# Tile 2 moves behind weight row 3 on SyncE's DMA queue, and weight row 6 takes its place on ScalarE's queue

## The chip, the cores and the metric

The kernel runs on one core of one Trainium2 chip. The metric is the device time of one execution in microseconds (us). The kernel before took 1615.66 us in the median of its first 3 runs (1615.08 to 1616.13). Only one core is used, so there is no other core to compare with.

PE is TensorE (the matrix engine), ACT is ScalarE, DVE is VectorE, SP is SyncE. "SPq" and "ACTq" are the sequencers of SyncE and ScalarE, which issue the DMAs. The span is the time from the first to the last instruction of a profiled execution; it is about 1.8 us shorter than the time.

## The reference

The program is two rounds of two layers, on an input of 2048 rows by 1024 columns in bfloat16:

```python
x = x + attention(layernorm(x), wqkv, wo)   # 8 dilated positions, 32 heads of 32
x = x + swiglu(layernorm(x), w1, w3, w2)    # hidden size 3584
# ... and both once more, with the same weights
```

Nearly all of the time is in the matrix multiplications (PE is busy 1601.8 of 1614.1 us). This study is about the first 16 us alone: the first 512 rows of `x` (tiles 0 to 3 of 128 rows each, 256 KB a tile) are normalized and multiplied by the Q part of `wqkv`. That part is loaded in 8 rows of 128 x 1024 (256 KB each); "row 6" is the seventh.

## The kernel before

Operations are first recorded with estimated durations. A small scheduler inside the kernel then puts them into one order for each engine, and the kernel emits them in that order. So a moved transfer can also change the order of much later instructions. `queue="AQ"` means that ScalarE issues the transfer; otherwise SyncE does.

The opening, with cuts:

```python
def q_first():
    for hh in range(2):                      # tile 0 in two halves, one on each queue
        dma(128, x_sb[0][...], xin[:, 0, ...], [], [("x", 0, hh)], 0, queue="AQ" if hh else "SP")
    dma(256, x_sb[1][:], xin[:, 1, :], [], [...], 0, queue="AQ")
    rows = q_weights(0, "k", load=False)
    for kk in range(5):
        rows[2](kk)                          # weight rows 0 to 4, SyncE
    load_x(0, 3, 4)                          # tile 3, SyncE
    rows[2](5)
    rows[2](7)
    # ... averages of tile 0: half on DVE, half on ACT (writes "part")
    dma(256, x_sb[2][:], xin[:, 2, :], [("part", 0)], [...], 0, queue="AQ")     # tile 2
    # ... average of tile 1 on ACT (writes mean 1)
    rows[2](6, queue="AQ", after=[("mean", 1)])                                 # row 6
    # ... tiles 0 and 1: subtract the mean, transpose on PE, copy to `ce`
    # ... tiles 2 and 3: statistics on DVE, normalize, transpose on PE, copy to `xnT`
    # PE, tiles 0 and 1 (line 520): one row of weights after another, kk = 0 .. 7
    # PE, tiles 2 and 3 (line 534): 64 matmuls, all weight rows
    # ...
    wslots[1] = q_weights(1, "s")            # K weights: two blocks of 1 MB, SyncE
```

PE's program order in this stretch is: rows 0 to 5 for tiles 0 and 1 (rows 0 to 2 first for tile 0, then for tile 1), row 6, the transposes of tiles 2 and 3 (line 430), row 7, then the 64 matmuls of tiles 2 and 3. The DMAs share eight completion semaphores in turn, so a DMA is issued only once the one eight places earlier has landed (in the first profile tile 3 at 4.88 us after row 0 at 4.87, row 6 at 6.76 after row 2 at 6.74). Row 6's issue stands in ScalarE's instruction order, behind a copy of tile 0.

## Time and profile before

| | kernel before |
|---|---|
| span of the profiled execution | 1614.1 us |
| PE busy | 1601.8 us |
| PE waits over 0.15 us | 2 (0.77 us at the start, 1.16 us for row 6) |
| row 6: issued, landed | 6.76, 12.98 us |
| matmuls of tiles 2 and 3 (line 534) start | 15.67 us |

The page's own totals, busy us and share of the span:

```profile
span 1614.1 us, 19082 instructions
PE 1601.8 (99%) x7463; PEld 762.8 (47%) x7610; DVE 1122.1 (70%) x1906; ACT 331.1 (21%) x527; POOL 5.3 (0%) x28
```

In this profile, 147 of PE's 7610 matmuls left no record. So the waits, and not the busy sum, say what PE loses. The waits of PE over the whole execution (who waited for whom: us in total, times, longest):

```profile
PE bank L520 <- DMA slot<-in_A_wqkv_dram: 1.2, 1, 1.2
PE bank L285 <- PEq L756: 0.8, 1, 0.8
```

The timeline of PE from 4 to 24 us (start, duration, what; in brackets the idle time before it and what ended it):

```profile
3.71 1.49 PE L285 MATMUL bank<-const-bfloat16-1.0 128*128 128x512 bf16 x3
4.99 0.69 PE L430 MATMUL bank<-ident,xn 128*128 128x128 bf16 x8
...
7.29 4.57 PE L520 MATMUL bank<-hT,slot 128*128 128x128 bf16 x56
13.02 1.05 PE L520 MATMUL bank<-hT,slot 128*128 128x256 bf16 x8 [1.16 <-DMA slot<-in_A_wqkv_dram]
13.91 1.06 PE L430 MATMUL bank<-ident,xn 128*128 128x128 bf16 x16
14.80 1.04 PE L520 MATMUL bank<-hT,slot 128*128 128x256 bf16 x8
15.67 7.15 PE L534 MATMUL bank<-xnT,slot 128*128 128x256 bf16 x64
```

And the chain of waits in the same stretch (start, us, what):

```profile
5.21 1.15 ACT xn L458 x2
6.36 0.40 ACT hT L435
6.76 6.22 DMA slot<-in_A_wqkv_dram
12.98 0.05 issue
13.02 1.05 PE bank L520 x8
```

PE is busy 99% of the time, and after 13 us it waits for nothing. The one avoidable wait is row 6's. It is 0.07% of the time, so the question from the start is one of a microsecond. The chain shows how the wait comes about: ACT averages tile 1 and copies, then issues row 6 at 6.76, and the transfer takes 6.22 us. Other 256 KB pieces took 3.7 to 5.1 us.

How the DMA engines are shared is seen in the DMA view of two short windows (queue, kind: packets, MB, share of 16 engines; q1 is SyncE's queue, q10 ScalarE's). From 4.9 to 6.4 us:

```profile
q1 hardware_dynamic: 305, 0.56, 102.9%
```

From 7 to 8 us:

```profile
q10 hardware_dynamic: 125, 0.23, 60.7%
q1 hardware_dynamic: 95, 0.16, 43.8%
```

Tile 2 was issued on ScalarE's queue at 3.67 us. From 4.9 to 6.4 us it moves nothing, while SyncE's queue moves 0.56 MB; the SyncE pieces that land next, rows 1 to 4 (5.79 to 8.10 us), were issued before it. Tile 2's bytes move from near 7 us on (60.7% for ScalarE's queue, 43.8% for SyncE's). Why they wait, these runs do not settle; nor does the trace show whether tile 2 already stood in its queue then. The engines are full (from 4 to 16 us their mean share is 105%, at 388 GB/s), and 256 KB pieces land 0.67 us apart (row 3 at 7.42 to row 7 at 10.80, six pieces). Row 6's bytes move late. From 10.5 to 12 us they are the only ones on ScalarE's queue and share the engines with SyncE's:

```profile
q1 hardware_dynamic: 172, 0.35, 63.1%
q10 hardware_dynamic: 124, 0.23, 41.7%
```

### The profile page before, as it was taken

The numbers are of one execution on the slowest core, as the hardware profiler recorded it, in microseconds if no ns is written. First come the engines' busy times: TensorE is split into PE (matmuls) and PEld (weight loads), VectorE is DVE, ScalarE is ACT, GpSimd is POOL, SyncE is SP. The second block draws the span as 40 slices with busy tenths as digits, with TensorE's granted clock in tenths as the row PEclk, the third lists the DMA queues.
The fourth block names the chain that finished last, engine by engine and source line by source line (L and its number), as shares of the span: only waits on it lengthen the run. The fifth ranks groups of instructions, "written<-read, shape, count | busy, mean of one in ns | idle before, by whom it ended". The sixth has DMA issues, their size and how long they took to land.

```text
span 1614.1 us, 19082 instructions
## 1 busy us (share of the span) xinstructions
PE 1601.8 (99%) x7463; PEld 762.8 (47%) x7610; DVE 1122.1 (70%) x1906; ACT 331.1 (21%) x527; POOL 5.3 (0%) x28
## 2 busy tenths in 40 slices
PE   9999999999999999999999999999999999999999
PEld 6555544444444444444444444444444444444444
DVE  5898888889889888888898729884288832211211
ACT  5423322021211222113211032110321101101110
POOL 1000000000000000000000000000000000000000
DMA  9834755395548764858545487355873464454451
GB/s 314 231 102 149 225 170 170 117 225 170 171 136 249 194 193 130 218 166 250 172 139 159 161 243 229 125 172 176 250 225 119 156 183 156 144 174 152 156 164 45
DMA packets 350649, 285.80 MB, mean 177 GB/s; under 512 B 72288, under 2 KB 344928, under 8 KB 350560
## 3 DMA queue, kind: packets, MB, share of 16 engines
q1 hardware_dynamic: 349984, 283.67, 58.5%
q8 instruction: 59, 0.97, 0.3%
q10 hardware_dynamic: 576, 0.92, 0.2%
q14 instruction: 30, 0.25, 0.1%
HBM read 238.94 MB, written 29.36 MB: 166 GB/s over the span
## 4 chain that ended last, share of the span: by engine, by line
PE 99%; DMA 1%; issue 0%; ACT 0%; DVE 0%; ACTq 0%
PE bank L347 98%; PE bank L534 0%; DMA slot<-in_A_wqkv_dram 0%; DMA x<-in_A_x_dram 0%; PE bank L520 0%; ACT xn L458 0%; PE bank L430 0%; ACT L281 0%; ACT hT L435 0%; DVE x L699 0%; ACTq L458 0%
## 5 line engine op out<-in xcount | busy, mean ns | idle before, releaser
L347 PE MATMUL bank<-xnT,slot 128*128 128x512 bf16 x4955 | 1088.9, 379 | 5.3
L347 PEld LDWEIGHTS <-slot 128*128 128x128 bf16 x5056 | 518.1, 102 | 573.0
L347 PE MATMUL bank<-slot,hT 128*128 128x512 bf16 (+2 forms) x1812 | 387.3, 372 | 1.9
L669 DVE TENSOR_TENSOR hT<-sg,bank 128x512 bf16<-128x512 bf16 x224 | 153.6, 686 | 212.6 <-PE bank L347 196.3
L265 DVE TENSOR_TENSOR scr<-scr 128x1024 bf16<-128x1024 bf16 (+3 forms) x576 | 293.7, 540 | 2.1
L347 PEld LDWEIGHTS <-hT 128*128 128x128 bf16 x1848 | 178.6, 98 | 208.6
L667 ACT ACTIVATE sg<-bank 128x512 bf16<-128x512 f32 x224 | 133.8, 597 | 654.1 <-PE bank L347 613.9
L265 DVE TENSOR_TENSOR scr<-qT,kT 128x2048 bf16<-128x2048 bf16 x128 | 154.2, 1221 | 72.4 <-DMA kT<-qkv_d 70.6
L405 ACT CAST sgt<-bank 128x512 bf16<-128x512 f32 x184 | 107.7, 587 | 288.4 <-PE bank L347 271.6
L265 DVE TENSOR_TENSOR scr<-pA,vT 128x2048 bf16<-128x2048 bf16 x128 | 152.9, 1222 | 0.4
L699 DVE TENSOR_TENSOR x<-x,bank 128x512 bf16<-128x512 bf16 (+1 forms) x66 | 43.7, 670 | 122.6 <-PE bank L347 122.4
L347 PE MATMUL bank<-wo,oT 128*128 128x512 bf16 x502 | 112.6, 379 | 0.5
L313 DVE BATCH_NORM_STATS2 st<-x 128x6 f32<-128x512 bf16 x124 | 81.6, 680 | 12.1 <-DMA x<-in_A_x_dram 11.7
L347 PEld LDWEIGHTS <-oT 128*128 128x128 bf16 x512 | 50.1, 98 | 60.4
L644 DVE TENSOR_TENSOR x<-x,bank 128x512 bf16<-128x512 bf16 x64 | 43.9, 686 | 35.4 <-PE bank L347 33.9
L320 ACT ACTIVATE sd<-mv,epst 128x4 f32<-128x4 f32 (+1 forms) x17 | 5.1, 298 | 183.0 <-DVE mv L316 182.7
L604 DVE STREAM_TRANSPOSE pB<-pA 128x2048 bf16<-128x2048 bf16 x16 | 37.0, 2310 | 0.4
L627 DVE STREAM_TRANSPOSE pA<-pB 128x2048 bf16<-128x2048 bf16 x16 | 37.0, 2310 | 0.4
L667 ACT ACT_TABLE_LOAD x20 | 25.7, 1283 | 51.0 <-PE bank L347 50.8
L265 DVE TENSOR_TENSOR pA<-scr 128x256 bf16<-128x256 bf16 x128 | 35.8, 287 | 0.3
L265 DVE TENSOR_TENSOR oT<-scr 128x256 bf16<-128x256 bf16 x128 | 34.2, 289 | 0.1
L327 DVE TENSOR_SCALAR xn<-x,mv,rstd 128x1024 bf16<-128x1024 bf16 x62 | 30.9, 542 | 4.0 <-DMA xnT<-xn 3.7
(61 smaller groups left out, 211.2 us busy)
## 6 DMA issues: line engine op xcount, KB each, us to landing
slot<-in_B_w_dram SPq DMA_DIRECT2D x160, 1024.0 KB, 5.9
slot<-in_A_wqkv_dram SPq DMA_DIRECT2D x28, 1024.0 KB, 5.2
qkv_d<-sgt SPq DMA_DIRECT2D x92, 256.0 KB, 3.4
qT<-qkv_d SPq DMA_DIRECT2D x16, 512.0 KB, 5.2
slot<-in_B_w_dram SPq DMA_DIRECT2D x16, 512.0 KB, 5.7
kT<-qkv_d SPq DMA_DIRECT2D x14, 544.0 KB, 6.7
vT<-qkv_d SPq DMA_DIRECT2D x14, 544.0 KB, 5.2
out_dram<-x SPq DMA_DIRECT2D x31, 128.0 KB, 4.2
```

The lines of the kernel that those rows point to most:

```text
L265: return lambda _: nc.vector.tensor_tensor(o, a, b, op=op)
L313: dve(0.67, lambda _, hh=hh: nc.vector.bn_stats(st[q][:, j, hh, :], x_sb[n][:, hh * 512:(hh + 1) * 512]), [("x", n, hh)] + list(after), [( ...
L320: act(0.3, lambda _: nc.scalar.activation(sd[q][:, j0:j1], mv[q][:, j0:j1, 1], ACTF.Sqrt, bias=epst[:]), [("mv", q, j) for j in range(j0, ...
L327: dve(0.5, lambda _: nc.vector.tensor_scalar(xn[j][:], x_sb[n][:], mv[q][:, j, 0:1], rstd[q][:, j:j + 1], op0=ALU.subtract, op1=ALU.mult), ...
L347: nc.tensor.matmul(bank[a.bank][:, 0:ncol], lhsT=w, rhs=r, start=first and i == 0, stop=last and i == n - 1)
L405: evac(act, 0.59, lambda _, a=a, i=i, m=m: nc.scalar.copy(sgt[i][:, m % 2, :], bank[a.bank][:]), op, [], [("sgt", i, m % 2)], a)
L604: dve(2.31, lambda _: nc.vector.transpose(psmT[:].rearrange("p c d -> p (c d)"), psm[:].rearrange("p w s -> p (w s)")), allA, ["pB"])
L627: dve(2.31, lambda _: nc.vector.transpose(At[:].rearrange("p w s -> p (w s)"), AeT[:].rearrange("p c d -> p (c d)")), ["pB"], allA)
L644: evac(dve, t1(512), lambda _, xs=xs, a=a: nc.vector.tensor_tensor(xs, xs, bank[a.bank][:], op=ALU.add), op, [("x", n, hh)], [("x", n, hh) ...
L667: evac(act, 0.6, lambda _, i=i, a=ag: nc.scalar.activation(sg[i][:], bank[a.bank][:], ACTF.Silu), og, [], [("sg", i)], ag, table="silu")
L669: evac(dve, t1(512), lambda _, i=i, a=au, f=f: nc.vector.tensor_tensor(hT[:, f, :], sg[i][:], bank[a.bank][:], op=ALU.mult), ou, [("sg", i ...
L699: evac(dve, t1(cn), lambda _, xs=xs, a=a, cn=cn: nc.vector.tensor_tensor(xs, xs, bank[a.bank][:, 0:cn], op=ALU.add), op, [("x", n, hh)], [ ...
```

## The change

The intent is to issue row 6 three microseconds earlier without delaying anything that PE needs sooner. Tile 2 is needed later than row 4 by PE (from 13.91 us against 9.96), and row 6 can take tile 2's old place, right after ACT has been given its half of tile 0's average.

```diff
-        for kk in range(5):
+        for kk in range(4):
             rows[2](kk)
+        load_x(0, 2, 3)
+        rows[2](4)
         load_x(0, 3, 4)
         rows[2](5)
         rows[2](7)
 # ... (cut)
-        dma(256, x_sb[2][:], xin[:, 2, :], [("part", 0)], [("x", 2, 0), ("x", 2, 1)], 0, queue="AQ")
+        rows[2](6, queue="AQ", after=[("part", 0)])
 # ... (cut: average of tile 1)
-        rows[2](6, queue="AQ", after=[("mean", 1)])
```

## The prediction

> **What bounds the kernel.** TensorE. The page gives PE 1601.8 of 1614.1 us busy, granted clock 1.000. By the waits view PE waits only twice: 0.8 us for the program's start, and 1.16 us (11.86 to 13.02) for a DMA of a Q-weight row. All other gaps are under 0.06 us. So no change of the opening can be worth more than about 1.3 us of 1615 (0.08%), however it goes.
>
> **What the wait is.** In the timeline of the first 26 us PE works the Q weights row by row: row 3 from 9.08, row 4 from 9.96, row 5 from 10.83; row 6 could start at 11.70 but starts at 13.02. Row 6 is issued on ScalarE's queue at 6.76 us, behind the averaging of tile 1 and a copy, when SyncE's queue already holds row 5, row 7 and two 1 MB blocks; it lands at 12.98, 6.2 us later. The DMA engines are full (about 395 GB/s from 4 to 16 us), and the 256 KB pieces land in one sequence 0.67 us apart on either queue: row 3 7.42 (SyncE), row 4 8.10 (SyncE), tile 2 8.78 (ScalarE), tile 3 9.45, row 5 10.12, row 7 10.80 (SyncE). [...]
>
> **What the change does.** Nothing is added or removed: the same transfers, matmuls and copies. The built programs show PE's order unchanged until about matmul 860 of 7610. Each DMA waits for an earlier one on its completion semaphore (eight, in turn). Row 6 takes tile 2's issue, 3.67 us; tile 2 takes row 4's; row 4 gets the wait that tile 3 had (for row 0, landing at 4.87), tile 3 that of row 5, and so on. So I estimate, in steps of 0.67 us: tile 2 lands at 8.1 (was 8.78), row 6 at 8.8 (was 12.98), row 4 at 9.45 (was 8.10), tile 3 at 10.1, row 5 at 10.8, row 7 at 11.5.
>
> **On the critical path.**
> - Row 6's wait vanishes: gain up to 1.32 us.
> - Row 4 lands 0.5 us before PE wants it (9.96). Row 5 lands just when PE wants it (10.83): cost 0 to 0.2 us.
> - VectorE's statistics of tile 2 finish earlier but its next instruction, tile 3's, starts about 0.13 us later (10.01 to 10.15). Tiles 2 and 3 are normalized at about 12.35 and 13.0, when PE finishes row 6 (12.6) and tile 2's transposes (13.05): cost 0 to 0.1.
> - The 64 matmuls of tiles 2 and 3 start at about 14.4 instead of 15.67.
>
> **Later.** PE then runs about 1.2 us earlier against DMA and VectorE. The scheduler also reorders later work: the output-projection groups move by 8 matmuls in 9 of 16 places. Before, VectorE finished their input 0.6 to 4.3 us ahead of PE. Some slack shrinks, so I allow 0.2 us of new short waits.
>
> **Predicted time:** 1614.5 us, 1613.4 to 1615.8 (runs of the kernel before scatter by about 0.5 us either way). Faster by over 2%: 0.003; within 2%: 0.992; slower: 0.005.
>
> **What would show it.** PE's wait for a weight row near 12 us is gone or below 0.3 us; row 6 lands near 8.8; row 4 near 9.5; tile 3's statistics start near 10.15; the matmuls of the second half of the Q stage start near 14.4; PE's busy time stays 1601.8 and the span falls by about 1.1.
>
> **What would make it wrong.** Row 5 landing well after 10.83, turning row 6's wait into row 5's; tile 3 late, so that PE waits for its transposes; new waits of PE for VectorE or a DMA after 100 us, where slack was small and the order changed. Each costs at most a few us: even then, the verdict is the same.

## The result, and the profile after

The changed kernel took 1615.05 us in the median of 6 runs (1614.84 to 1615.30), the kernel before 1615.81 us in the same rounds (1614.98 to 1616.57). The ratio is 0.9996, with a 95% interval of 0.9983 to 1.0009: the same time by the 2% rule. A ratio is the mean time of one kernel's fast runs over that of the other's of the same rounds, so it is not quite the ratio of the medians.

The page's totals of the changed kernel:

```profile
span 1613.1 us, 19082 instructions
PE 1601.3 (99%) x7463; PEld 762.7 (47%) x7610; DVE 1122.3 (70%) x1906; ACT 329.6 (20%) x526; POOL 5.3 (0%) x28
```

All waits of its PE:

```profile
PE bank L285 <- PEq L757: 0.8, 1, 0.8
PE bank L430 <- DVE xn L472: 0.4, 1, 0.4
PE bank L521 <- DMA slot<-in_A_wqkv_dram: 0.2, 1, 0.2
```

The same timeline of PE (the changed kernel's line numbers are one higher here: 521 for 520, 535 for 534):

```profile
3.71 0.92 PE L285 MATMUL bank<-const-bfloat16-1.0 128*128 128x512 bf16 x3
4.53 0.72 PE L430 MATMUL bank<-ident,xn 128*128 128x128 bf16 x8
5.19 0.61 PE L521 MATMUL bank<-hT,slot 128*128 128x128 bf16 x8
5.96 0.62 PE L521 MATMUL bank<-hT,slot 128*128 128x128 bf16 x8 [0.16 <-DMA slot<-in_A_wqkv_dram]
6.96 0.66 PE L430 MATMUL bank<-ident,xn 128*128 128x128 bf16 x8 [0.39 <-DVE xn L472]
7.46 5.44 PE L521 MATMUL bank<-hT,slot 128*128 128x128 bf16 x64
12.74 1.06 PE L430 MATMUL bank<-ident,xn 128*128 128x128 bf16 x16
13.63 1.04 PE L521 MATMUL bank<-hT,slot 128*128 128x256 bf16 x8
14.51 7.15 PE L535 MATMUL bank<-xnT,slot 128*128 128x256 bf16 x64
```

The 56 matmuls before the wait and the 8 after it are now one run of 64, without a gap: row 6's wait is gone. The last group starts at 14.51 instead of 15.67, which is 1.16 us earlier, and the span is 1.0 us shorter. Two small waits are new, 0.16 us for row 1 and 0.39 us for tile 1's mean. Both stand before row 2. In this execution PE also began 0.46 us earlier (4.53 instead of 4.99): the last three of its ten warm-up matmuls on constants (line 285) took 0.92 us instead of 1.49. Tile 0 landed earlier too, at 3.08 us rather than 3.46, but that does not explain it alone: in profile c of the kernel before, below, tile 0 landed at 3.08 and PE began at 4.99. That the Q group is earlier by just the 1.16 us of the old wait is therefore partly chance: PE gained 0.46 us at the start and lost 0.55 in the two new waits. In the changed kernel's second profile PE began at 4.99, and the Q group at 14.82.

The chain of waits no longer contains a weight row:

```profile
6.55 0.36 DVE xn L472
6.92 0.05 issue
6.96 0.66 PE bank L430 x8
7.62 5.28 PE bank L521 x64
```

Where each piece landed, from the trace, beside the prediction:

| piece | before | predicted | changed kernel |
|---|---|---|---|
| tile 2 | 8.78 | 8.1 | 8.43 |
| row 6 | 12.98 | 8.8 | 8.62 |
| row 4 | 8.10 | 9.45 | 9.28 |
| tile 3 | 9.45 | 10.1 | 9.97 |
| row 5 | 10.12 | 10.8 | 10.63 |
| row 7 | 10.80 | 11.5 | 11.29 |

### The profile page after: what moved, and what is told of

It reads as the page before. It is cut to its first block, busy times and chain, and to the rows that moved or that the text cites. A ratio compares the mean times of both kernels' runs of the same rounds, so it can differ in the third digit from the quotient of the medians.

```text
span 1613.1 us, 19082 instructions
## 1 busy us (share of the span) xinstructions
PE 1601.3 (99%) x7463; PEld 762.7 (47%) x7610; DVE 1122.3 (70%) x1906; ACT 329.6 (20%) x526; POOL 5.3 (0%) x28
## 4 chain that ended last, share of the span: by engine, by line
PE 99%; issue 1%; DMA 0%; ACT 0%; DVE 0%; ACTq 0%
PE bank L347 98%; PE bank L535 0%; PE bank L521 0%; DMA x<-in_A_x_dram 0%; PE bank L430 0%; ACT L281 0%; DVE xn L472 0%; ACT xn L460 0%; DVE x L700 0%; ACTq L460 0%
```

## The experiments

Two questions were open. First, does the microsecond come from the opening alone, or also from the changed order of later work? Second, why did row 6 take 6.2 us, and why do the runs of the kernel before scatter by 1.6 us when those of the changed kernel scatter by 0.5? Each run below was timed in 5 rounds beside the kernel before (nine runs of it in each batch), except the last three.

### The changed kernel again

No edit.

> The changed kernel as it stands, for comparison on this chip. Theory A (the removed 1.16 us wait is passed on to the end nearly whole): 0.6 to 1.3 us below the kernel before; no PE wait for a weight row over 0.3 us. Rival B (the difference seen so far is chance; something later takes the gain back): within 0.4 us of the kernel before.

Measured: 1615.26 us (1615.09 to 1615.37); the kernel before 1615.63 us (1614.66 to 1617.65), ratio 0.9996 (0.9984 to 1.0009). PE has no wait for a row above 0.15 us. By the medians the gain is 0.37 us, which is the rival's range; by the means it is larger (0.56 us), because the kernel before has runs above 1617. So the changed kernel is not faster than the best runs of the kernel before: it lacks the slow ones.

### The opening alone, and the later order alone

For the first, the list that the scheduler made of the kernel before is kept, and only the two transfers are moved in it:

```diff
+        placed = pr.place()
+        # r6, x2, r3: the operations that load row 6, tile 2, row 3
+        placed.remove(r6)
+        placed[placed.index(x2)] = r6
+        placed.insert(placed.index(r3) + 1, x2)
+        x2.emit = lambda _: nc.sync.dma_start(x_sb[2][:], xin[:, 2, :])
-        for op in pr.place():
+        for op in placed:
             op.emit(op)
```

> The changed kernel's opening (tile 2 behind row 3 on SyncE's queue, row 6 in its place on ScalarE's), with every later instruction in the order of the kernel before. Theory A (only the opening counts): equal to the changed kernel within 0.3 us, so 0.6 to 1.3 us below the kernel before. Rival C (the later reordering brings or costs time): off the changed kernel by 0.5 us or more.

Measured: 1615.03 us (1614.87 to 1615.16), ratio to the kernel before 0.9995 (0.9983 to 1.0008). It is 0.23 us from the changed kernel's median in the same batch. In its profile PE waits for no row; up to 5.42 us it waits 1.0 us for tile 0, whose second half landed at 4.17 us instead of 3.64.

The second is the mirror image: the changed kernel's list, with tile 2 put back on ScalarE's queue and row 6 put back behind ACT's first copy and behind the first 1 MB block in the list.

> The opening of the kernel before (row 6 issued late on ScalarE's queue), with every later instruction in the order of the changed kernel. Theory A: equal to the kernel before within 0.3 us, PE waits about 1.2 us for row 6 near 12 us. Rival C: 0.5 us or more off the kernel before.

Measured: 1615.21 us (1614.92 to 1616.05), ratio 0.9998 (0.9985 to 1.0010). Its profiled run, the slowest of the five, has PE waiting 0.97 us for row 6 and a span of 1614.2 us. Its median is 0.42 us below that of the kernel before, a little more than A allowed, at a scatter of over 1 us in both. Together the two runs leave no room for a cost or gain of the later order above about 0.4 us. The traces say it more sharply. In all profiled executions, from the start of the last Q group (line 534) to the end takes 1598.4 to 1598.65 us, whichever order is used. Whatever the opening gains or loses reaches the end.

### Half of the change: tile 2 alone

Tile 2 goes behind row 3 on SyncE's queue; row 6 stays where it was.

```diff
-        for kk in range(5):
+        for kk in range(4):
             rows[2](kk)
+        load_x(0, 2, 3)
+        rows[2](4)
 # ... (cut)
-        dma(256, x_sb[2][:], xin[:, 2, :], [("part", 0)], [("x", 2, 0), ("x", 2, 1)], 0, queue="AQ")
```

> Half of the change: tile 2 goes behind row 3 on SyncE's queue, row 6 stays at its late place on ScalarE's queue (issued near 6.8 us). Theory A (row 6's issue time is what counts): row 6 still lands near 13 us and PE waits 0.9 to 1.3 us for it; time within 0.4 us of the kernel before. Rival D (tile 2's earlier arrival gives the gain): most of the gain, 0.6 us or more, is there.

Measured: 1616.06 us (1615.03 to 1616.86), ratio 1.0001 (0.9987 to 1.0015). Row 6 is issued at 6.95 and lands at 12.95; PE waits 1.08 us for it. Tile 2 lands at 8.26 instead of 8.78, and that is worth nothing: the median is 0.43 us above that of the kernel before, just past A's limit of 0.4. The gain is row 6's.

### Row 6 one step later

To double the suspected wait, row 6 is issued after ACT's second copy (of tile 1).

```diff
-        rows[2](6, queue="AQ", after=[("mean", 1)])
 # ... (cut: the transposes of tiles 0 and 1)
+        rows[2](6, queue="AQ", after=[("ce", 1, 7)])
```

> The kernel before with row 6 issued one step later on ScalarE's queue (near 7.6 us, after the second copy of tile 1), behind both 1 MB K-weight blocks in order of issue. Theory A (PE's wait for row 6 is passed on whole): the time rises by as much as PE's wait near 12 us grows. How much, tells two pictures of the DMA engines apart. G (pieces move in order of issue whatever the queue): row 6 lands after the first block at least, at 14 to 18 us, PE waits 2.5 us or more and the time is 1.3 us or more above the kernel before. H (the two queues share evenly as soon as both have work): row 6 lands by 13.8 us, wait under 2.1 us, time within 1 us of the kernel before.

Measured: 1618.48 us (1617.18 to 1620.06), ratio 1.0018 (1.0005 to 1.0031), the only ratio here that is clear of 1. Row 6 is issued at 7.65, after both blocks (7.17 and 7.64), and lands at 13.84. PE waits 2.06 us for it:

```profile
13.89 1.85 PE L520 MATMUL bank<-hT,slot 128*128 128x256 bf16 x8 [2.06 <-DMA slot<-in_A_wqkv_dram]
```

It had also waited 0.43 us for row 1. So landing and wait are those of H (to within 0.04 us), and the row landed before the first block (15.52), which G excludes. But the time, 3.3 us above the kernel before, is not H's: theory A's "passed on whole" would give about 0.9 us more than in the kernel before's first profile, and the span is 2.5 us longer. The missing part is PE's clock. The windows view (each engine's busy time in a stretch, the column PEclk being the granted clock):

```profile
core 0: us, PE busy (x) PEld busy (x) DVE busy (x) ACT busy (x) POOL busy (x), PEclk, DMA share, GB/s
10.55:11.80 1.25, 1.25 (x12) 0.89 (x10) 1.22 (x6) 0.48 (x2) 0.00 (x0) 1.00 0.96 360
11.80:13.90 2.10, 0.04 (x2) 0.02 (x2) 1.74 (x8) 0.48 (x2) 1.11 (x5) 1.00 1.03 348
13.96:17.37 3.41, 3.41 (x25) 2.90 (x26) 0.74 (x2) 0.59 (x1) 2.06 (x12) 0.50 1.37 316
17.37:20.78 3.41, 3.41 (x33) 3.04 (x32) 0.57 (x2) 3.13 (x6) 0.00 (x0) 1.00 0.67 131
```

Right after the wait the granted clock is 0.50 for 3.41 us. From the start of row 6 to the start of the last Q group takes 4.29 us (13.89 to 18.18) instead of 2.65 (13.02 to 15.67): 1.64 us more. With row 6 itself 0.87 us later, that makes the 2.5 us. Waits of 1.08 and 0.97 us (tile 2 alone, later order alone) left the mean granted clock at 1.000, and from row 6 to the Q group took 2.65 us in both. From what length of wait on the clock falls, these runs do not show. This is one profile. Of the five runs, three have a mean clock of 0.999 and two 1.000, one of them (1618.48 us) as slow as the profiled one (1618.42).

### The two 1 MB blocks held

Row 6 keeps its late place. VectorE writes one column into the K-weight slot after its copy of tile 1, so that the blocks are issued only then; their operations are moved behind row 6 in the list.

```diff
+        placed[at:at] = [k0, k1]     # behind row 6
         for op in placed:
             op.emit(op)
+            if op is h1:             # VectorE's copy of tile 1
+                nc.vector.memset(slot[2][:, 0:1], 0.0)
```

> The kernel before, row 6 still at its late place on ScalarE's queue (6.3 to 6.8 us), but the two 1 MB K-weight blocks on SyncE's queue held about 1 us (to about 7.7 us) by a one-column write of VectorE into their slot. Theory E (row 6 is late because it is issued at the moment of the first 1 MB block and shares the engines with it; which goes first differs from run to run, and that is the scatter of the kernel before): row 6 lands near 11.5, PE waits at most 0.3 us, time like the changed kernel (near 1615.1) and scatter as small as its. Rival F (the late issue, or ScalarE's queue, is enough by itself): row 6 still lands at 12.5 or later, PE waits 0.8 us or more, time and scatter as of the kernel before.

Measured: 1615.34 us (1615.18 to 1615.48), ratio 0.9997 (0.9984 to 1.0009); row 6 lands at 11.69, and PE has no wait for it. As a test it failed: with the block behind it, row 6 got another semaphore's turn and was issued at 5.97 instead of 6.76. Two things were changed, and the run does not tell them apart. The last-but-one experiment below repairs this.

### Row 6 early without moving tile 2

Either on SyncE's queue between rows 5 and 7, or on ScalarE's queue behind tile 2:

```diff
-        rows[2](6, queue="AQ", after=[("mean", 1)])
+        rows[2](6)                                      # run A: between rows[2](5) and rows[2](7)
+        rows[2](6, queue="AQ", after=[("part", 0)])     # run B: right behind tile 2
```

First run A:

> The kernel before with tile 2 untouched and row 6 on SyncE's queue between rows 5 and 7. Theory G (order of issue): row 6 lands near 10.8, row 7 near 11.5; PE has no wait for a row over 0.2 us; time like the changed kernel within 0.3 us. Rival (the swap of tile 2 and row 6, or ScalarE's queue for row 6, is needed): PE waits 0.5 us or more near 12 us or later, time 0.5 us or more above the changed kernel.

Measured: 1615.09 us (1614.74 to 1615.29), ratio 0.9995 (0.9983 to 1.0008); row 6 is issued at 6.16 and lands at 10.49, and PE waits for nothing. Then run B:

> The kernel before with tile 2 untouched and row 6 issued behind it on ScalarE's queue at about 5.3 us instead of 6.8, ahead of row 5. Theory G: row 6 lands near 10.1, row 5 near 10.8, row 7 near 11.5; PE waits under 0.3 us for a row; time like the changed kernel within 0.3 us. Rival (being behind tile 2 on ScalarE's queue is what holds row 6): row 6 lands after 11.7, PE waits.

Measured: 1614.99 us (1614.79 to 1615.11), ratio 0.9995 (0.9981 to 1.0009); row 6 is issued at 5.19 and lands at 10.43. PE waits for nothing. So neither the swap with tile 2 nor a particular queue is needed. These two have the shortest spans of the profiled executions (1613.0 us), but by time they are not told apart from the changed kernel.

### Row 6 late, with the blocks held

Row 6 is at the place of "one step later", and VectorE's column is written after the first statistics of tile 2, so the blocks come after row 6 for certain.

```diff
-        rows[2](6, queue="AQ", after=[("mean", 1)])
+        rows[2](6, queue="AQ", after=[("ce", 1, 7)])    # as above
 # ... (cut: the two blocks are moved in the list as in the held run above, here behind s2)
+            if op is s2:             # first statistics of tile 2
+                nc.vector.memset(slot[2][:, 0:1], 0.0)
```

> Row 6 issued as late as in the run before with row 6 one step later (about 7.5 us, later than in the kernel before), but the two 1 MB blocks held until VectorE has done the first statistics of tile 2 (about 9.5 us), so that none of them is issued ahead of row 6. Theory E (what holds row 6 is the 1 MB block issued ahead of it): row 6 lands by 12.0, PE waits at most 0.4 us, time within 0.4 us of the changed kernel (1614.8 to 1615.5), small scatter. Rival F (the late issue alone is enough): row 6 lands at 13 or later, 5.5 us or more after its issue; PE waits 1.2 us or more; time 1616 or more.

Measured: 1614.95 us (1614.87 to 1615.71), ratio 0.9994 (0.9980 to 1.0007). Row 6 is issued at 7.96, 1.2 us later than in the kernel before, and lands at 12.07 (E had said by 12.0), 0.9 us earlier. PE does not wait for it; after tile 1's transposes its 64 matmuls up to row 6 run without a gap:

```profile
7.75 5.45 PE L520 MATMUL bank<-hT,slot 128*128 128x128 bf16 x64
```

(The profiled run, the slowest of the five, lost 0.45 us to row 1, which landed at 6.80, and some more to tile 2, which landed at 9.78. Had PE come to row 6 at 11.86, as in the first profile, it would by our estimate have waited some 0.25 us, still within E's 0.4.) So a late issue alone does not make the wait. What makes it is a 1 MB block issued ahead of row 6 or together with it, though not every time, as the next profiles show: issued later but ahead of the blocks, the row took 4.1 us instead of 6.2.

### The kernel before, three more profiles

No edit; the question is why its runs differ.

> The kernel before once more, for another profile of it. Theory E: its span follows the landing of row 6: 11.5 to 12 gives a span near 1613.2, 13 gives 1614.1, later than 13.7 gives 1615.5 or more with a drop of the granted clock. Rival (the scatter comes from the later 1590 us): the span does not follow row 6's landing; PE has other waits.

> As the run before: a further profile of the kernel before; same expectations.

> As the two runs before: a further profile of the kernel before; same expectations.

Measured, with the first profile beside them and the other late kernels below (all us; "wait" is PE's wait for row 6, by the gaps of its timeline; "Q group" is the start of the 64 matmuls of tiles 2 and 3):

| execution | 1st block issued | row 6 issued | row 6 landed | wait | Q group | span |
|---|---|---|---|---|---|---|
| before, first profile | 6.66 | 6.76 | 12.98 | 1.16 | 15.67 | 1614.1 |
| before, a | 6.69 | 6.75 | 12.12 | 0.07 | 14.82 | 1613.3 |
| before, b | 6.53 | 6.65 | 12.78 | 0.83 | 15.48 | 1613.9 |
| before, c | 6.88 | 6.69 | 11.97 | 0 | 14.76 | 1613.2 |
| later order alone | 6.81 | 7.25 | 13.09 | 0.97 | 15.79 | 1614.2 |
| tile 2 alone | 6.62 | 6.95 | 12.95 | 1.08 | 15.64 | 1614.3 |
| row 6 later | 7.17 | 7.65 | 13.84 | 2.06 | 18.18 | 1616.6 |
| row 6 later, blocks held | 10.53 | 7.96 | 12.07 | 0 | 15.27 | 1613.9 |
| changed kernel | 7.25 | 3.31 | 8.62 | 0 | 14.51 | 1613.1 |

In execution c, row 6 was issued before the block, and PE waited for nothing. The waits of PE in that execution of the unchanged kernel are:

```profile
PE bank L285 <- PEq L756: 0.8, 1, 0.8
```

The span follows the start of the Q group in every line to within 0.2 us, and within the kernel before it follows row 6's landing. In the kernel before the issue of row 6 waits for row 2's landing (6.74, issued 6.76 in the first profile). The block's turn comes when SyncE has issued rows 5 and 7, and row 5 waits for row 1's landing (5.79, issued 5.81). Two landings thus race to decide which goes first. The order of issue is not all of it: in execution a the block was issued 0.06 us ahead, and PE still waited only 0.07 us. The DMA view splits the four as the landings do. Here is the share of ScalarE's queue, which then holds row 6 alone, from 9 to 10.5 us, in the first profile and in a:

```profile
q10 hardware_dynamic: 9, 0.02, 3.2%
q10 hardware_dynamic: 101, 0.20, 36.1%
```

In b it is 4.5% and in c 40.3%. So when the two are issued within 0.2 us of each other, row 6's bytes move either before 10.5 us or mostly after; what settles it then, these runs do not show. The changed kernel issues row 6 some four microseconds before the block, and there is no race left.

The times show it too. Over all batches the kernel before was run 36 times: 1614.66 to 1620.41 us, mean 1615.86, median 1615.45, with 5 runs above 1617. The changed kernel was run 11 times: 1614.84 to 1615.37, mean 1615.14, median 1615.15. (These pool several batches, not always the same chip.) The two slowest runs of the kernel before, 1620.41 and 1619.59 us, have a mean granted clock of 0.999, as the profiled run with row 6 later has (0.50 for 3.41 us is 0.1% of the span). That they were slow by the same drop of clock is likely, but no profile of such a run was caught, so it is argued and not shown. The three others above 1617 us have 1.000, and the waits of the four profiles (at most 1.16 us) do not explain them; they stay open.

## Why the prediction was right or wrong

**"No change of the opening can be worth more than about 1.3 us": right for the profiled execution, not for all.** The wait was avoidable in full, and from the Q group on nothing moved by more than 0.2 us. The measured gain was 0.76 us between the medians of the first comparison and 0.71 us between the means of all runs. But the kernel before has slow runs up to 5 us above its median, which the changed kernel did not show in 11 runs. The bound left out that a longer wait can be followed by a lower PE clock, as in the run with row 6 later (0.50 for 3.41 us after a wait of 2.06 us).

**"Row 6's wait vanishes: gain up to 1.32 us": the mechanism right, the size one draw.** The wait vanished, and the Q group began 1.16 us earlier. The prediction took 1.16 us as the wait of the kernel before. Four profiles of that kernel show 1.16, 0.07, 0.83 and 0 us. The mis-sized term is this one: its mean over the four is 0.5 us, which fits that the medians moved less than the 1.1 us predicted for them.

**"It lands 6.2 us later", behind row 5, row 7 and two 1 MB blocks: right in kind.** The block issued at the same moment can stretch it, as the late row with held blocks showed (4.1 us). The second block was not yet issued in the first profile (7.44 against 6.76).

**The landings in steps of 0.67 us: right within 0.35 us for all six pieces**, as the table of landings shows; only row 6 landed 0.19 us after tile 2 and not a whole step. Row 5, called the closest, landed at 10.63, and PE did not wait for it.

**VectorE's statistics and the transposes: right.** The Q group started at 14.51 (predicted 14.4), and PE waited for no transpose of tiles 2 and 3.

**"I allow 0.2 us of new short waits" later: none came.** From the Q group to the end took 1598.4 to 1598.65 us in every profile, and both ends of that range occur with either later order. The new waits, 0.39 and 0.16 us, came in the opening instead, at tile 1 and row 1; the prediction had not named them.

**The time: 1614.5 predicted, range 1613.4 to 1615.8, measured 1615.05: right**, as was "within 2%". The range held because it allowed for scatter, not because the scatter was understood: the prediction called 0.5 us either way noise of the runs, and by the four profiles part of it was this very wait.

## What to carry to other kernels

A transfer that the matrix engine needs soon should be issued before any large transfer that it does not need yet, on either queue. Here row 6, issued by 6.16 us on SyncE's or by 5.19 us on ScalarE's, landed by 10.49 us and PE did not wait for it; issued within 0.2 us of a 1 MB block, it landed at 11.97 to 12.98 us and made PE wait anything from 0 to 1.2 us. Where a kernel's runs scatter, profile it several times before costing a wait from one trace: the wait may be a race, and removing it shows more in the slow runs than in the median. Keep waits of a busy matrix engine short for a second reason: in the one profile of it, a wait of 2.06 us was followed by a granted clock of 0.50 for 3.41 us, which cost another 1.64 us.
